# A top-32 attention with two MLPs on one core: K and V buffers assigned by next use, head pairs in alternating order, 28 weight low halves on GpSimd, and the instruction list made by two more backward and forward passes

## The chip, the core and the metric

The kernel runs on one core of one Trainium2 chip. Times are microseconds (us) on the device, from the launch of the program to its end on that core. The median of three runs of the kernel before is 1062.55 us. One further execution was profiled; its own time is 1063.52 us, and the profile's span, from its first to its last instruction, is 1061.7 us.

## The reference

Attention over 4 batches, 8 heads, 576 tokens and 64 columns, in which each query keeps its 32 largest scores; then an MLP with ELU; then a gated MLP whose third product has no nonlinearity behind it.

```python
scores = scale * np.matmul(q, k.transpose(0, 1, 3, 2))
kth = np.partition(scores, -top_k, axis=-1)[..., -top_k:-top_k + 1]
scores = np.where(scores >= kth, scores, -1000000000.0)
...
attn = attn / (np.sum(attn, axis=-1, keepdims=True) + 1e-09)
x = np.matmul(attn, v)                  # to (2304, 512)
h = x @ w_in                            # 512 x 2048
g = np.where(h > 0.0, h, alpha * (np.exp(np.minimum(h, 0.0)) - 1.0))
y = g @ w_out                           # 2048 x 512
h = (y @ w1) * (y @ w2) @ w3            # 512 x 1024 twice, 1024 x 1024
return h @ w_out2                       # 1024 x 512
```

## The kernel before

**Work and tiles.** The 2304 tokens are 18 tiles of 128, taken in 9 chunks of 2. For a chunk, attention goes over the 4 pairs of heads and, within a pair, over the 2 tiles. A step of attention on one tile and pair is: load q (line 288, from 410 on), split it into a high and a low part on ScalarE and GpSimd (L414, L415), score matmuls on TensorE (L435), evacuation by ScalarE (L437), the top 32 on VectorE as four MAX8 and three MATCH_REPLACE8 per head (L445, L447), mask and exponential on ScalarE (L460, L462), split of the probabilities (L470 on ScalarE, L471 on GpSimd), transposes by DMA (L473), the product with V (L488), the division and split (L499 to L509) and a transpose into X (L510). A tile that straddles two batches takes K and V of both.

**The MLPs** of a chunk follow its attention by one chunk. Unit A is x·W_in (L747 to L749, three f16 products for each f32 one: high·high, high·low, low·high), with the ELU on ScalarE and GpSimd (L759 to L771); unit O is g·W_out (L784 to L786); Y evacuates (L796, L797); unit B is the two gated products (L826 to L828) and their product on VectorE (L836 to L852); unit D is the product with W34 = W3·W_out2 (L861 to L863), and the output goes out. W34 is computed once, by the 64 f32 products of L686.

**Weights.** They arrive as 8-byte words and are made f32 by `load64` (two ScalarE steps, L539 and L541, one of VectorE, L540, one of GpSimd, L542). The tensors w12 and w34 serve as landing places before they hold their own weights. `convert` (L561) then splits a 128x512 tile into two f16 halves: the high half always on ScalarE (L566), the low half in a mode that `conv_modes` picks for every tile. In mode P, TensorE forms scaled weight minus high half in PSUM (L578, L579) and VectorE or ScalarE evacuates it (L582). In mode D, VectorE does it in one instruction (L569). Before, W_in and W_out (16 tiles each) are all P with the evacuation on VectorE; W34 (8 tiles) and W12 (16 tiles) are all D.

**K and V.** There are three K buffers (KT) and four V buffers (VV). `att_loads` and `v_loads` take the next buffer in turn. The first time a batch and pair of heads are needed they are loaded raw (kd, vd), converted (K: L357 and L358; V: L379 and L382), and the converted tile is stored to DRAM (KD, VD); every later time it is reloaded from there. Inside a chunk a K tile that still stands in its buffer is not reloaded.

**Order.** No instruction is placed by hand. `Program.op` collects all operations with an engine, an estimated cost and the buffers they read and write. `emit` (L125) then simulates the engines: at each point the engine that is free first takes, of its operations that are ready, the one of lowest rank. The rank comes from a due time, offsets by group (OFF) and the length of the path behind it. Each engine then runs its instructions in the order so found, waiting on semaphores; the SP engine issues all DMAs, also in order.

Of the kernel before, what the change touches and what calls it, by code (L numbers as in the profile page):

```python
# [39 lines left out]
OFF = {":DVE": 13807, "A0:ACT": -12479, "A0:PE": 9089, "A0:POOL": 28926, "A1:ACT": 1887, "A1:PE": 1481, "A1:POOL": -6842, "A2:ACT": 12564, "A2:PE":  # L40
# [53 lines left out]
class Program:  # L94
# [29 lines left out]

    def emit(self):  # L125
        n = len(self.ops)
        succ = [[] for _ in range(n)]
        miss = [0] * n
        for i, o in enumerate(self.ops):
            miss[i] = len(o[3])  # L130
# [857 lines left out]
```

## Time and profile before

| | |
|---|---|
| median of 3 runs (lowest, highest) | 1062.55 us (1062.33, 1064.52) |
| the profiled execution: own time, span | 1063.52 us, 1061.7 us |
| busy in the span: TensorE, VectorE, ScalarE, GpSimd | 978.0, 888.4, 826.1, 695.2 us |
| mean granted TensorE clock | 0.974 |
| moved by DMA | 174.97 MB |

Busy time is the union of an engine's instructions. The granted clock is a share of 2.4 GHz; 0.5 is 1.2 GHz. A stretch A:B runs from A to B in us from the span's start.

### The profile page before, as it was taken

What the parts mean: (1) busy time and instruction counts of PE and PEld (TensorE: products, weight loads), DVE (VectorE), ACT (ScalarE), POOL (GpSimd) and SP (SyncE); (2) the same over time, 40 slices, a digit from 0 to 9 for tenths busy, and PEclk for the clock granted to TensorE, in tenths of its full rate; (3) what the DMA queues carried; (4) which work ended last, traced back from release to release, by engine and by line L of the source; (5) the groups of instructions that cost most, each with busy time, mean ns of one, the idle gap of its engine ahead of it and who ended that gap; (6) DMA issues with size and microseconds to landing.
All of it is one profiled execution on the core that took longest, in us unless ns stands there. A gap on an engine that the chain in (4) does not pass through costs nothing.

```text
span 1061.7 us, 24618 instructions
## 1 busy us (share of the span) xinstructions
PE 978.0 (92%) x9132; PEld 776.7 (73%) x9132; DVE 888.4 (84%) x1968; ACT 826.1 (78%) x1521; POOL 695.2 (65%) x743
## 2 busy tenths in 40 slices
PE   3486998988899999999999999999999999999998
PEld 2334454777787788977888888788778968978875
DVE  4999998999999999999979999997999999710011
ACT  6899987898999767978887788899669877824512
POOL 4968665698478646965884587489457856833702
PEclk9598999999999999999999999999999999999999
DMA  9979997689456985488787536865862663320000
GB/s 356 397 223 289 304 273 171 192 209 236 118 161 153 238 192 120 90 193 212 187 227 174 147 76 176 221 188 140 179 154 65 138 151 70 57 51 21 1 20 20
DMA packets 255384, 174.97 MB, mean 165 GB/s; under 512 B 196640, under 2 KB 223264, under 8 KB 255264
## 3 DMA queue, kind: packets, MB, share of 16 engines
q1 hardware_dynamic: 255264, 173.41, 63.2%
q8 instruction: 71, 1.16, 0.5%
q14 instruction: 49, 0.40, 0.1%
HBM read 104.56 MB, written 21.61 MB: 119 GB/s over the span
## 4 chain that ended last, share of the span: by engine, by line
PE 33%; DVE 26%; ACT 16%; DMA 11%; POOL 6%; issue 6%; SPq 1%; DVEq 0%; ACTq 0%; POOLq 0%
DVE m L445 10%; DVE wk L447 8%; PE psR L826 2%; PE psR L827 2%; PE psR L828 2%; PE psY L784 2%; DMA raw<-kd 2%; PE psY L786 2%; PE psY L785 2%; DMA qr<-qd 2%; DMA pt<-pi 2%; PE psR L747 2%; PE psR L748 2%; PE psR L749 2%; PE psY L686 2%
## 5 line engine op out<-in xcount | busy, mean ns | idle before, releaser
L445 DVE MAX8 m<-wk 128x8 f32<-128x576 f32 x432 | 311.2, 746 | 0.8
L471 POOL TENSOR_TENSOR pi<-s,pi 128x576 f16<-128x576 f32 x144 | 185.9, 1298 | 80.3 <-ACT pi L470 57.1
L447 DVE MATCH_REPLACE8 wk<-m,wk 128x576 f32<-128x576 f32 x288 | 212.3, 740 | 0.0
L747 PE MATMUL psR<-x,win 128*128 128x256 f16 x576 | 157.2, 273 | 5.9 <-ACT t L768 5.6
L785 PE MATMUL psY<-g,wout 128*128 128x256 f16 x576 | 158.1, 275 | 3.3 <-POOL g L771 3.3
L784 PE MATMUL psY<-g,wout 128*128 128x256 f16 x576 | 158.5, 275 | 1.1 <-ACT g L770 1.1
L826 PE MATMUL psR<-x,w 128*128 128x256 f16 x576 | 158.0, 274 | 1.2 <-DVE t L846 0.9
L786 PE MATMUL psY<-g,wout 128*128 128x256 f16 x576 | 158.1, 274 | 0.0
L827 PE MATMUL psR<-x,w 128*128 128x256 f16 x576 | 157.6, 274 | 0.0
L828 PE MATMUL psR<-x,w 128*128 128x256 f16 x576 | 157.5, 273 | 0.0
L749 PE MATMUL psR<-x,win 128*128 128x256 f16 x576 | 157.0, 273 | 0.0
L748 PE MATMUL psR<-x,win 128*128 128x256 f16 x576 | 157.0, 273 | 0.0
L435 PE MATMUL psS<-kt,qh 128*128 128x288 f32 x320 | 111.7, 363 | 19.5 <-ACT s L437 18.4
L460 ACT ACTIVATE s<-s,m 128x576 f32<-128x576 f32 x144 | 108.6, 770 | 23.4 <-DVE m L445 23.2
L437 ACT ACTIVATE s<-psS 128x576 f32<-128x576 f32 (+1 forms) x160 | 102.9, 643 | 16.4 <-PE psS L435 9.7
L445 DVE MAX8 m<-s 128x8 f32<-128x576 f32 x144 | 104.5, 744 | 10.5 <-ACT s L437 10.3
L462 ACT ACTIVATE s<-s,ty 128x576 f32<-128x576 f32 x144 | 106.7, 769 | 4.4 <-POOL ty L456 4.4
L447 DVE MATCH_REPLACE8 wk<-m,s 128x576 f32<-128x576 f32 x144 | 106.1, 740 | 0.0
L470 ACT ACTIVATE pi<-s 128x576 f16<-128x576 f32 x144 | 95.0, 676 | 8.7 <-DMA pt<-pi 8.1
L769 POOL TENSOR_TENSOR t<-t,t 128x512 f32<-128x512 f32 x72 | 92.8, 1290 | 5.5 <-ACT t L768 3.8
L415 POOL TENSOR_TENSOR ql<-qr,qh 128x256 fp32r<-128x256 f32 x72 | 54.1, 752 | 60.8 <-ACT qh L414 57.0
L435 PE MATMUL psS<-kt,ql 128*128 128x288 f32 x320 | 93.4, 305 | 0.1
(155 smaller groups left out, 2382.6 us busy)
## 6 DMA issues: line engine op xcount, KB each, us to landing
kt<-kd SPq DMA_DIRECT2D x32, 576.0 KB, 4.6
vv<-vd SPq DMA_DIRECT2D x32, 455.0 KB, 4.6
qr<-qd SPq DMA_DIRECT2D x72, 128.0 KB, 3.0
raw<-kd SPq DMA_DIRECT2D x32, 288.0 KB, 3.8
kd<-kt SPq DMA_DIRECT2D x16, 576.0 KB, 4.6
w<-w_in SPq DMA_DIRECT2D x16, 512.0 KB, 5.9
w<-w_out SPq DMA_DIRECT2D x16, 512.0 KB, 6.9
w<-w3t SPq DMA_DIRECT2D x16, 512.0 KB, 5.5
```

The lines of the kernel that those rows point to most:

```text
L435: T.matmul(psS[:, half, 0:288], lhsT=L[qs][:, hh], rhs=KT[kk][:, hh, half * 288:half * 288 + 288], start=li == 0, stop=li == 1)
L445: op("DVE", 665, lambda r=r, src=src, m8=m8, hh=hh: V.max(m8[:, hh, 8 * r:8 * r + 8], src), [skey], [mk], p1 + PAR["ot"] * STEP)
L447: op("DVE", 727, lambda r=r, src=src, w=w, m8=m8, hh=hh: V.match_replace(w, m8[:, hh, 8 * r:8 * r + 8], src, -3.0e38), [skey, mk], [k], p1 ...
L471: op("POOL", 1240, lambda Y=Y, PIs=PIs, hh=hh: G.tensor_tensor(PIs[:, hh, S:2 * S], Y[:, hh], PIs[:, hh, 0:S], op=OP.subtract), hks, [pk], ...
L747: T.matmul(o, lhsT=hi(W)[:, cs], rhs=X[:, 0, kd_, 0:N], start=kd_ == 0, stop=False)
L748: T.matmul(o, lhsT=hi(W)[:, cs], rhs=X[:, 1, kd_, 0:N], start=False, stop=False)
L784: T.matmul(o, lhsT=hi(W)[:, cs], rhs=rh, start=ft == 0 and m % 2 == 0, stop=False, skip_group_check=True)
L785: T.matmul(o, lhsT=hi(W)[:, cs], rhs=rl, start=False, stop=False, skip_group_check=True)
L786: T.matmul(o, lhsT=lo(W)[:, cs], rhs=rh, start=False, stop=ft == 15, skip_group_check=True)
L826: T.matmul(o, lhsT=hi(W)[:, cs], rhs=X[:, 0, kd_, 0:N], start=kd_ == 0, stop=False)
L827: T.matmul(o, lhsT=hi(W)[:, cs], rhs=X[:, 1, kd_, 0:N], start=False, stop=False)
L828: T.matmul(o, lhsT=lo(W)[:, cs], rhs=X[:, 0, kd_, 0:N], start=False, stop=kd_ == 3)
```

## The change

1. **Buffers by next use.** A new `plan` walks the known sequence of uses of K and V ahead of time. If a tile still stands in a buffer, it is a hit and nothing is loaded. Else it takes the buffer whose content is needed furthest in the future. Only tiles that will be loaded again are stored.
2. **Pairs in alternating order.** Odd chunks take the four pairs from the last to the first (`snake=1`).
3. **Low halves by GpSimd alone.** A new mode S scales the f32 tile in place on GpSimd and subtracts the high half there. 6 of 16 tiles of W_in, 6 of 16 of W_out, all 8 of W34 and 8 of 16 of W12 take it, 28 in all. The other 20 tiles of W_in and W_out stay P, the other 8 of W12 stay D.
4. **The list.** The forward simulation of `emit` becomes a function. Its result is refined twice: a backward pass from the finish times gives every operation a latest start, and the next forward pass ranks operations by that.
5. All offsets in OFF have other values. The new parameter `blag` is 0, so `hold`, `bprev` and the `Bp` units do nothing here.

```diff
-PAR = dict(hv={}, lv={'wi': 16, 'wo': 16}, whole=(), cd={'wi': [0, 0], 'wo': [0, 0], 'w34': [8, 0], 'w12': [16, 0]}, ...
+PAR = dict(fb=2, snake=1, blag=0, hv={}, lv={'wi': 16, 'wo': 16}, whole=(), cd={'wi': [0, 0, 6], 'wo': [0, 0, 6], 'w34': [0, 0, 8], 'w12': [8, 0, 8]}, ...
...
-OFF = {":DVE": 13807, "A0:ACT": -12479, ...
+OFF = {":DVE": 17768, "A0:ACT": -31993, ...
...
-def conv_modes(n, d, g):
+def conv_modes(n, d, g, s=0):
...
+    for z, mode in ((g, "G"), (s, "S")):
+        free = [i for i in range(n) if m[i] == "P"]
+        for k in range(min(z, len(free))):
+            m[free[k * len(free) // z]] = mode
...
+    def backward(self, succ, fin):
...
+            while wait[e] and wait[e][0][0] <= t:
+                _, i = heapq.heappop(wait[e])
+                heapq.heappush(ready[e], (-fin[i], i))
+            _, i = heapq.heappop(ready[e])
+            eng, cost, fn, deps, pr, lat, lk = self.ops[i]
+            free[e] = t + (max(cost, lat) if e == "SP" else cost)
+            end = free[e] + (1100.0 if e == "SP" else 0.0)
+            late[i] = -end
...
+        cur = self.forward(succ, rank)
+        for _ in range(PAR["fb"]):
+            cur = self.forward(succ, self.backward(succ, cur[2]))
+        self.length, order, _ = cur
...
+    def pairs(c):
+        return range(4) if c % 2 == 0 or not PAR["snake"] else range(3, -1, -1)
+
+    def plan(n, uses):
+
+        last, homes, seen, again, steps = {}, [None] * n, set(), set(), []
+        for i, u in enumerate(uses):
+            for x in u:
+                last.setdefault(x, []).append(i)
+        for i, u in enumerate(uses):
+            for x in u:
+                if x in homes:
+                    steps.append((homes.index(x), "hit"))
+                    continue
+                far = [-1 if h in u else len(uses) + n - k if h is None else min([j for j in last[h] if j > i], default=len(uses)) for k, h in enumerate(homes)]
+                k = far.index(max(far))
+                homes[k] = x
+                if x in seen:
+                    again.add(x)
+                steps.append((k, "again" if x in seen else "first"))
+                seen.add(x)
+        return iter(steps), again
...
     def att_loads(b, p, pr):
-        ks = nxt("k", NK)
-        if ("k", b, p) in seen:
+        ks, how = next(kplan)
+        if how == "hit":
+            return ks
+        if how == "again":
             dma(KT[ks].rearrange("p a s -> p (a s)").bitcast(I32), KD[b, p].bitcast(I32), 128 * S * 8, [("kd", b, p)], [("k", ks)], pr)
             return ks
...
-        dma(KD[b, p], KT[ks].rearrange("p a s -> p (a s)").bitcast(F32), 128 * S * 8, [("k", ks)], [("kd", b, p)], pr + PAR["ost"] * STEP)
+        if (b, p) in kagain:
+            dma(KD[b, p], KT[ks].rearrange("p a s -> p (a s)").bitcast(F32), 128 * S * 8, [("k", ks)], [("kd", b, p)], pr + PAR["ost"] * STEP)
...
-        for pair in range(4):
+        for at, pair in enumerate(pairs(c)):
...
-        if mode == "G":
-            op("ACT", 570, lambda: A.activation(st, st, AF.Copy, scale=s), [sk], skeys, pr)
+        if mode in "GS":
+            if mode == "G":
+                op("ACT", 570, lambda: A.activation(st, st, AF.Copy, scale=s), [sk], skeys, pr)
+            else:
+                op("POOL", 660, lambda: G.tensor_scalar(st, st, s, 1.0, op0=OP.mult, op1=OP.mult), [sk], skeys, pr)
             op("POOL", 1160, lambda: G.tensor_tensor(lo(W[i]), st, hi(W[i]), op=OP.subtract), [*skeys, (nm, i)], [(nm, i, "l")], pr)
             return
```

`v_loads` changes as `att_loads` does. In the lists below a row is a line, an operation and its tiles; L542 of before is L623 of the change, L471 is L552, L415 is L498, L456 is L537, L771 is L855, L762 is L846, L769 is L853; L656 and L657 are the two steps of mode S.

The first place is GpSimd's list before W34 is begun, where the last tiles of W_out become f32 (win, wout, w34: weight tiles; w12: landing place; ql, qh: split q; pi, s: probabilities; ty: thresholds). Before:

```order
L542 TENSOR_TENSOR w34_100<-w34_100,w12_99 128x512 x4
L542 TENSOR_TENSOR wout_98<-wout_98,w12_99 128x512 x2
L415 TENSOR_TENSOR ql1_108<-qr_104,qh1_106 128x256
L471 TENSOR_TENSOR pi0_121<-s0_116,pi0_121 128x576
L542 TENSOR_TENSOR wout_98<-wout_98,w12_99 128x512 x2
L471 TENSOR_TENSOR pi0_121<-s0_116,pi0_121 128x576
L456 TENSOR_TENSOR ty1_147<-m81_143 128x2
L542 TENSOR_TENSOR wout_98<-wout_98,w12_99 128x512 x2
L415 TENSOR_TENSOR ql0_107<-qr_104,qh0_105 128x256
L542 TENSOR_TENSOR wout_98<-wout_98,w12_99 128x512 x5
```

and now:

```order
L498 TENSOR_TENSOR ql1_108<-qr_104,qh1_106 128x256
L623 TENSOR_TENSOR wout_98<-wout_98,w12_99 128x512
L552 TENSOR_TENSOR pi0_121<-s0_116,pi0_121 128x576
L623 TENSOR_TENSOR wout_98<-wout_98,w12_99 128x512
L656 TENSOR_SCALAR win_97<-win_97,sc_96 128x512
L623 TENSOR_TENSOR wout_98<-wout_98,w12_99 128x512
L657 TENSOR_TENSOR win_97<-win_97 128x512
L656 TENSOR_SCALAR win_97<-win_97,sc_96 128x512
```

Between the W_out tiles stand now the low halves of W_in (L656, L657), five such pairs in all with those that follow these rows; a probability split that stood there comes later.

The second place is GpSimd's list near the end of chunk 0's first layer, where W12's last tiles become f32 (pp: its last two landing places; g, t: the ELU's tiles; xt: attention's output). Before:

```order
L542 TENSOR_TENSOR pp_138<-pp_138 128x512
L762 TENSOR_SCALAR t4_131<-t4_131,sc_96 128x512
L771 TENSOR_TENSOR g0_132<-t2_129,g0_132 128x512
L471 TENSOR_TENSOR pi0_121<-s2_118,pi0_121 128x576
L769 TENSOR_TENSOR t4_131<-t4_131,t0_127 128x512
L471 TENSOR_TENSOR pi0_121<-s2_118,pi0_121 128x576
L771 TENSOR_TENSOR g1_133<-t4_131,g1_133 128x512
L542 TENSOR_TENSOR pp_138<-pp_138 128x512
L415 TENSOR_TENSOR ql0_107<-qr_104,qh0_105 128x256
L456 TENSOR_TENSOR ty3_149<-m83_145 128x2
```

and now:

```order
L846 TENSOR_SCALAR t4_131<-t4_131,sc_96 128x512
L853 TENSOR_TENSOR t4_131<-t4_131,t0_127 128x512
L552 TENSOR_TENSOR pi0_121<-s2_118,pi0_121 128x576
L656 TENSOR_SCALAR w12_99<-w12_99,sc_96 128x512
L590 TENSOR_TENSOR xt0_135<-xf0_137,xt0_135 128x128
L623 TENSOR_TENSOR pp_138<-pp_138 128x512
L657 TENSOR_TENSOR w12_99<-w12_99 128x512
L537 TENSOR_TENSOR ty3_149<-m83_145 128x2
L855 TENSOR_TENSOR g0_132<-t2_129,g0_132 128x512
L855 TENSOR_TENSOR g1_133<-t4_131,g1_133 128x512
L656 TENSOR_SCALAR w12_99<-w12_99,sc_96 128x512
```

Low halves of W12 (w12_99 in L656 and L657) follow directly, between the last ELU steps and the next probabilities.

The third place is SP's list while W3 is loaded (qr: query; raw: K or V as it comes; kt, kd0, vv, vd0: converted tiles in SBUF and DRAM; pt, x0: transposes). Before:

```order
L288 DMA qr_104<-qd 128x2x128
L288 DMA kt2_111<-kd0_1_64 128x1152
L473 DMA_TRANSPOSE pt0_122<-pi0_121 128x9x128
L288 DMA raw_101<-vd 128x512
L288 DMA w12_99<-w3t 128x4x256
L288 DMA kd0_3_66<-kt0_109 128x1152
L288 DMA w12_99<-w3t 128x4x256
L288 DMA vv0_112<-vd0_0_79 128x1820
L473 DMA_TRANSPOSE pt0_122<-pi0_121 128x9x128
L288 DMA vd0_3_82<-vv3_115 128x1820
```

and now:

```order
L554 DMA_TRANSPOSE pt1_123<-pi0_121 128x9x128
L337 DMA w12_99<-w3t 128x4x256 x4
L554 DMA_TRANSPOSE pt1_123<-pi0_121 128x9x128
L554 DMA_TRANSPOSE pt0_122<-pi0_121 128x9x128
L337 DMA raw_101<-kd 128x576
L337 DMA w12_99<-w3t 128x4x256
L337 DMA qr_104<-qd 128x2x128
L591 DMA_TRANSPOSE x0_124<-xt0_135 128x2x128
L337 DMA raw_101<-vd 128x640
L337 DMA w12_99<-w3t 128x4x256 x2
L554 DMA_TRANSPOSE pt0_122<-pi0_121 128x9x128
```

The stores and reloads of K and V in between are gone; the W3 pieces follow each other and the transposes more closely.

## Rows read from the trace of the kernel before

**Rows 1.** The page: its head and part 1, busy us (share) xinstructions of each engine.
```profile
span 1061.7 us, 24618 instructions
PE 978.0 (92%) x9132; PEld 776.7 (73%) x9132; DVE 888.4 (84%) x1968; ACT 826.1 (78%) x1521; POOL 695.2 (65%) x743
```

**Rows 2.** Table by stretches (us): length, busy us (xinstructions) of PE, PEld, DVE, ACT, POOL; clock; DMA share, GB/s.
```profile
0.00:195.00 195.00, 147.00 (x713) 78.06 (x714) 177.18 (x377) 164.30 (x292) 128.13 (x129) 0.89 0.93 280
195.00:270.00 75.00, 64.88 (x742) 56.46 (x740) 72.61 (x162) 67.99 (x127) 65.08 (x65) 0.98 0.84 214
195.00:384.00 189.00, 171.06 (x1828) 145.38 (x1826) 182.98 (x398) 170.29 (x315) 140.56 (x145) 0.97 0.76 193
384.00:944.00 560.00, 545.91 (x5682) 464.14 (x5680) 518.58 (x1169) 453.12 (x851) 389.39 (x433) 1.00 0.62 147
944.00:1062.00 118.00, 113.99 (x916) 89.08 (x914) 9.70 (x27) 38.42 (x65) 37.17 (x37) 0.99 0.04 15
40.00:121.00 81.00, 61.36 (x300) 30.53 (x301) 80.58 (x174) 78.13 (x140) 59.05 (x53) 0.83 0.95 294
121.00:195.00 74.00, 69.81 (x325) 36.29 (x325) 71.17 (x152) 58.09 (x107) 44.00 (x48) 0.98 0.87 218
201.00:368.00 167.00, 151.25 (x1608) 128.11 (x1607) 163.39 (x355) 154.69 (x285) 129.60 (x134) 0.98 0.73 183
```

**Rows 3.** Single lines: count, duration ns min/median/max, first and last start us.
```profile
L686 PE MATMUL psY<-w,pp x128: 590/592/1061, 121.1 to 194.3; 128*128 128x512 f32 x128
L747 PE MATMUL psR<-x,win x576: 269/273/286, 194.7 to 999.4; 128*128 128x256 f16 x192
L488 PE MATMUL psA<-vv,pt x2240: 189/193/262, 83.8 to 942.8; 128*128 128x65 f16 x105, 128*128 128x64 f16 x46, 128*64 128x65 f16 x24, 128*64 128x64 f16 x12
L762 POOL TENSOR_SCALAR t<-t,sc x72: 687/695/1284, 201.4 to 1001.5; 128x512 f32<-128x512 f32 x72
```

**Rows 4.** PE in order of time, last chunk of tokens.
```profile
984.03 0.27 PE L784 MATMUL psY<-g,wout 128*128 128x256 f16 x1
984.14 0.27 PE L785 MATMUL psY<-g,wout 128*128 128x256 f16 x1
```

**Rows 5.** Who PE waited for from 384 to 944: us in total, times, longest.
```profile
PE psS L435 <- ACT s L437: 5.0, 9, 1.2
PE psA L488 <- DMA pt<-pi: 4.3, 6, 1.5
```

**Rows 6.** PE in order of time: start us, us, instruction; conversions at half and full clock.
```profile
54.63 1.92 PE L578 MATMUL psY<-win,si 128*128 128x512 f32 x2
56.77 0.60 PE L578 MATMUL psY<-win,si 128*128 128x512 f32 x1
...
117.70 1.10 PE L578 MATMUL psY<-w,si 128*128 128x512 f32 x2
118.86 1.02 PE L578 MATMUL psY<-w,si 128*128 128x512 f32 x2
```

**Rows 7.** Groups of instructions: xcount | busy us, mean ns | idle before.
```profile
L771 POOL TENSOR_TENSOR g<-t,g 128x512 f16<-128x512 f32 x72 | 84.0, 1168 | 8.3 <-ACT g L770 6.5 <-issue 1.3
L762 POOL TENSOR_SCALAR t<-t,sc 128x512 f32<-128x512 f32 x72 | 50.8, 706 | 19.8 <-ACT t L760 19.0
L569 DVE SCALAR_TENSOR_TENSOR w<-w,sc 128x512 f16<-128x512 f32 x21 | 21.5, 1046 | 0.2
L582 DVE CAST win<-psY 128x512 f16<-128x512 f32 x16 | 11.0, 685 | 0.2 <-PE psY L579 0.2
```

**Rows 8.** GpSimd in order of time: the last step of chunk 1's first layer.
```profile
367.76 1.16 POOL L771 TENSOR_TENSOR g<-t,g 128x512 f16<-128x512 f32 x1 [1.34 <-issue]
```

**Rows 9.** The page, part 6, DMA issues: xcount, KB each, median us to landing.
```profile
kt<-kd SPq DMA_DIRECT2D x32, 576.0 KB, 4.6
vv<-vd SPq DMA_DIRECT2D x32, 455.0 KB, 4.6
```

More of the change, by code (lines that the diff above doesn't have):

```diff
@@ L123, in op, with forward @@
         self.groups.append(f"{self.tag}:{eng}")
[L125 removed]
+    def forward(self, succ, rank):
         n = len(self.ops)
[L127 to L130, printed above, removed]
[L131 to L137 removed]
+        miss = [len(o[3]) for o in self.ops]
         engs = sorted({o[0] for o in self.ops})
@@ L182, in emit @@
                 end = free[e] = t + cost
+            fin[i] = end
             for s in succ[i]:
@@ L187, in emit @@
                     heapq.heappush(wait[self.ops[s][0]], (rt[s], s))
+        return max(free.values()), order, fin
+    def backward(self, succ, fin):
+        n = len(self.ops)
+        miss = [len(s) for s in succ]
+        engs = sorted({o[0] for o in self.ops})
+        free = {e: 0.0 for e in engs}
+        wait = {e: [] for e in engs}
+        ready = {e: [] for e in engs}
+        rt = [0.0] * n
+        late = [0.0] * n
+        for i in range(n):
+            if miss[i] == 0:
+                heapq.heappush(wait[self.ops[i][0]], (0.0, i))
+        for _ in range(n):
+            best = None
+            for e in engs:
+                if ready[e]:
+                    t = free[e]
+                elif wait[e]:
+                    t = max(free[e], wait[e][0][0])
+                else:
+                    continue
+                if best is None or t < best[0]:
+                    best = (t, e)
+            t, e = best
+            while wait[e] and wait[e][0][0] <= t:
[6 more added lines that the diff above has]
+            late[i] = -end
+            for d in deps:
+                de = self.ops[d][0]
+                rt[d] = max(rt[d], end + (900.0 if de == "SP" else LAT.get((de, eng), 130.0)))
+                miss[d] -= 1
+                if miss[d] == 0:
+                    heapq.heappush(wait[de], (rt[d], d))
+        return late
@@ new lines, in emit @@
+    def emit(self):
+        n = len(self.ops)
+        succ = [[] for _ in range(n)]
+        for i, o in enumerate(self.ops):
+            for d in o[3]:
+                succ[d].append(i)
+        cp = [0.0] * n
+        for i in range(n - 1, -1, -1):
+            e, c = self.ops[i][:2]
+            cp[i] = c + max([cp[s] + (2050.0 if e == "SP" else LAT.get((e, self.ops[s][0]), 130.0)) for s in succ[i]], default=0.0)
+        rank = [o[4] - PAR["cpw"] * cp[i] for i, o in enumerate(self.ops)]
+        cur = self.forward(succ, rank)
+        for _ in range(PAR["fb"]):
+            cur = self.forward(succ, self.backward(succ, cur[2]))
+        self.length, order, _ = cur
@@ L188, in emit @@
         order.sort()
-        self.length = max(free.values())
-        self.busy = {e: sum(o[1] for o in self.ops if o[0] == e) for e in engs}
+        self.busy = {e: sum(o[1] for o in self.ops if o[0] == e) for e in {o[0] for o in self.ops}}
         for _, i in order:
@@ L344 @@
     op("DVE", 135, consts, [], ["ident", ("xf", 0), *[(k, i) for k in ("v", "vl") for i in range(NV)]], -1e6)
+    def pairs(c):
[9 more added lines that the diff above has]
+                    steps.append((homes.index(x), "hit"))
+                    continue
+                far = [-1 if h in u else len(uses) + n - k if h is None else min([j for j in last[h] if j > i], default=len(uses)) for k, h in enumerate(homes)]
[6 more added lines that the diff above has]
+        return iter(steps), again
+    starts = [sum(chunks[:i]) for i in range(len(chunks))]
+    kuse, vuse = [], []
+    for c_, n_ in enumerate(chunks):
+        for p_ in pairs(c_):
+            for t_ in range(starts[c_], starts[c_] + n_):
+                kuse.append([(b_, p_) for b_ in range(t_ * 128 // S, (t_ * 128 + 127) // S + 1)])
+            vuse.append([(b_, p_) for b_ in sorted({starts[c_] * 128 // S, ((starts[c_] + n_) * 128 - 1) // S})])
+    kplan, kagain = plan(NK, kuse)
+    vplan, vagain = plan(NV, vuse)
     def att_loads(b, p, pr):
-        ks = nxt("k", NK)
-        if ("k", b, p) in seen:
+        ks, how = next(kplan)
+        if how == "hit":
+            return ks
+        if how == "again":
             dma(KT[ks].rearrange("p a s -> p (a s)").bitcast(I32), KD[b, p].bitcast(I32), 128 * S * 8, [("kd", b, p)], [("k", ks)], pr)
             return ks
-        seen.add(("k", b, p))
         for hh in range(2):
@@ L877, in mlp @@
         dp = list(dprev)
+        seq += [("Bp", b) for b in bprev]
         if dp:
@@ L882, in mlp @@
             seq.append(("Dp", dp.pop(0)))
-        for j in range(8):
-            seq.append(("B", j))
+        if not hold:
+            for j in range(8):
+                seq.append(("B", j))
         for kind, i in seq:
             pr = pr_of(u)
-            c_ = c - (kind == 'Dp')
+            c_ = c - (kind in ("Dp", "Bp"))
             P.tag = f"{kind[0]}{c_ if c_ < 4 or c_ > len(chunks) - 3 else chr(115)}"
@@ L900, in mlp @@
                 i(pr)
-                u += 1
+                u += kind == "Dp"
             u += kind != "Y"
-        return [lambda pr, t=t: unitD(t, pr) for t in range(n)]
-    starts = [sum(chunks[:i]) for i in range(len(chunks))]
+        ds = [lambda pr, t=t: unitD(t, pr) for t in range(n)]
+        return (ds, [lambda pr, j=j: unitB(j, pr) for j in range(8)]) if hold else ds
     prep_v(0, PAR["pv"] * STEP)
@@ L911 @@
     st12 = prep_12(PAR["p12"] * STEP)
+    done12 = []
     def hooks(kind, i):
-        if kind == "Y":
+        if not done12 and (kind == "Bp" or kind == "Y" and not PAR["blag"]):
+            done12.append(1)
             for f in finish_12(st12, (PAR["p12"] + 16 * PAR["p12s"]) * STEP):
                 f()
-    dprev = []
+    dprev, bprev = [], ()
     for c, n in enumerate(chunks):
@@ L929 @@
             banks[:] = [0, 1] if c == 1 else [0, 1, 2]
-            dprev = mlp(c - 1, starts[c - 1], m, dprev, (starts[c] * 8 + PAR["lag0" if c == 1 else "lag"]) * STEP, m * 8 * STEP, hooks if c == 1 else None)
+            banks[:] = [0, 1] if c == 1 + PAR["blag"] else banks
+            hold = c == 1 and PAR["blag"] == 1
+            dprev = mlp(c - 1, starts[c - 1], m, dprev, (starts[c] * 8 + PAR["lag0" if c == 1 else "lag"]) * STEP, m * 8 * STEP, hooks if c < 3 else None, bprev, hold)
+            bprev = ()
+            if hold:
+                dprev, bprev = dprev
     c = len(chunks) - 1
```

51 lines of the change are left out of this document (20 added, 31 removed), and 56 rows, old and new, of the table OFF.

## Prediction

> **What bounds the kernel now.** I read the page first [rows 1]: TensorE (PE) is busy 978.0 of 1061.7 us, VectorE (DVE) 888.4, so no share of busy time decides by itself; the stages must be taken apart. The table by stretches does that [rows 2], with the cuts at the milestones of [rows 3]: the first product W3·W4 at 121.1, the first matmul of chunk 0's MLP at 194.7, the last attention product at 942.8.
> - 384 to 944: PE is busy 545.9 of 560, DVE 518.6. The f16 matmuls start 0.11 us apart although each row says 0.27 [rows 4]; they overlap, and "busy" here means that the next is already queued. PE is the limit, DVE close behind. PE idles 14.1 us; its two largest waits there are for score evacuations (5.0) and for the transposes of the probabilities (4.3) [rows 5].
> - 944 to the end: attention is over, PE works off what is queued, 114.0 of the last 117.7 us.
> - 0 to 195: PE has 48 us of idle time. From 40 to 121 DVE is busy 80.6 of 81 and ScalarE (ACT) 78.1, while GpSimd (POOL) has 22 us free and the TensorE clock is granted at 0.83 on average, so part of it at 1.2 GHz. DVE and ACT pace the weight conversion, and with it the start of everything.
> - 195 to 384: all four are loaded. PE idles 17.9, DVE 6.0, ACT 18.7, POOL 48.4.
>
> So the end moves by what comes off PE's work plus what changes in PE's idle time. A microsecond of PE work removed in the front counts only if DVE and ACT let PE use it.
>
> The Trainium skill's page "Perfetto Trace Analysis" (Identifying the Most-Contended Engine) says that matmul occupancy does not measure how full TensorE is. By that alone 92% would prove no bound, and PE work taken away might be worth nothing, which is the first rival's time; the overlap in [rows 4] shows why the page warns, and the even spacing there is why I keep the bound.
>
> **The change, part by part.**
> *28 low halves.* Twelve leave PE and DVE: a conversion on PE is a pair of f32 passes and one f16 matmul, and the next begins 1.16 us later at full clock (117.70 to 118.86), 2.14 at half (54.63 to 56.77) [rows 6]. 12 x 1.16 = 13.9 us of PE work go (25.7 if all ran at half clock). DVE loses 12 evacuations of 0.69 and 16 direct low halves of 1.05 [rows 7]: 8.2 + 16.7 = 24.9 us. POOL gains 28 pairs; the scaling has the shape of L762 (0.71), the subtraction that of L771 (1.17) [rows 7]: 28 x 1.87 = 52.5 us. The shortest and longest L762, 0.69 and 1.28 [rows 3], bound a pair between 1.86 and 2.45, so 52 to 69. I take 52.5, since the median is at the low end.
>
> *Front, to the first W3·W4 product.* In the new lists ACT has 14 attention and K/V instructions fewer and 3 weight instructions more ahead of the second W3 piece: 11 x 0.56 (78.13 us over 140 instructions [rows 2]) = 6.1 us. DVE sheds more (the 12 evacuations alone are 8.2), so ACT decides. POOL has 10 pairs more there, 18.7 us, less six attention or K instructions that now come later; its 22 free us hold that. I take **-6**. Of the 13.9 us off PE the other 8 become idle time. Ends: 0 (if another wait takes over) and -13.9. The block of 64 products that follows is PE-bound (busy 69.8 of 74 from 121 to 195 [rows 2]), so it moves as a whole. The lists have the same 27 score steps, 8 attention products and all but one W3·W4 product ahead of the first MLP matmul, so nothing else is owed at that point.
>
> *195 to 384.* 16 pairs (29.9 us) fall between the first POOL step of chunk 0's MLP and the last of chunk 1's first layer, from 201 [rows 3] to 368 [rows 8], where POOL has 37.4 us free [rows 2]. They replace DVE's 16.7 us. DVE is the fuller engine here, and the score and attention work waits on it. I let PE's 17.9 idle us fall by **4**; ends -17.9 and, if POOL cannot fit the work, the second rival below.
>
> *K and V.* K reloads fall from 32 to 12 and K stores from 16 to 12; V reloads from 32 to 6 and V stores from 16 to 6. A store carries the same tile as a reload; by the sizes in [rows 8], 24 x 576 + 36 x 455 KB = 30.9 MB no longer move. Transposes share the engines with them, and PE waits 4.3 us for transposes after 384. The two passes over the list aim at the same idle time. Together **-3** from 384 to 944; ends 0 and -9.3, the sum of the two waits in [rows 5]. The new wait: all reloads still wait for the last score step on their buffer, SP issues in order, and a late one holds up the query loads and transposes queued behind it. One reload lands in 4.6 us [rows 9]; a K tile serves two query tiles, so one wait that long is covered while the other tile's top-32 runs. I cost it at nothing and leave it to the second rival's side of the range.
>
> *Tail.* Seven of the D steps (six matmuls each) now stand ahead of the last attention product; this shifts work, PE stays full, 0.
>
> **Sum.** Own time of the profiled execution 1063.5 - 6 - 4 - 3 = 1050.5. The median of the runs is 1.0 lower, so **1049.5**. The ends of the terms add up to 1021 below and, with the second rival, 1070 above; they would all have to fall together.
>
> **Rivals.**
> 1. *Nothing reaches the end.* The front is paced by ACT, which loses no instruction at all, and the freed PE time is all idle. If more conversions fall into stretches at 1.2 GHz, as part of 40 to 121 is now, each costs 0.98 more and eats up the rest. For: 78.1 of 81 busy. Against: the list in front of the W3 pieces is shorter on ACT and DVE both. Time 1062.
> 2. *POOL becomes the limit* between the first and second chunk's first layer. In 201 to 368 POOL works 129.6; with 29.9 more it is 159.5. In 195 to 270, when it always had work, it was busy 65.1 of 75, 87%. At that rate 159.5 takes 184 us, 17 more than now; 6 earlier at the start and 3 recovered later leave +8: **1070**. It decides once POOL cannot hold 159.5/173 = 92%. For: POOL waits mostly for ACT, which is just as full. Against: a low half waits only for its high half, so it fills gaps. The Trainium skill's "GPSIMD Engine Reference" (Engine selection) speaks for this rival: it wants elementwise work with two inputs on VectorE, as GpSimd needs about twice as long. The rows agree in direction (1.17 against 0.69 in [rows 7], with other operands): on the engines' own clocks the change pays 52.5 us for 24.9 plus 13.9, a loss wherever POOL is what the others wait for.
> 3. *The passes do more than I grant.* Half of PE's 32 idle us after 195 vanish and all 13.9 us of PE work come off: 1062.5 - 13.9 - 16 = 1033. For: the new list interleaves finer. Against: PE stands at 97% after 384 already.
> That the change does not do what it says is closed: the instruction counts above are from the lists.
>
> **Numbers.** About 0.2%, 2.1 us, is what a measurement of this kernel can tell from no change. The forecast has 0.70 (1037 to 1059), the first rival 0.10, the second 0.09, the third 0.11. The range 1036 to 1063 leaves out the second rival and about two thirds of the third. Faster: 0.70 + 0.11, less a little at the edge, 0.80; same 0.10; slower 0.10.
>
> **What would show it.** Right: 20 conversions on PE; the first W3·W4 product near 115 and the first MLP matmul near 188; POOL over 90% busy for the 160 us after that with PE no more idle than before; last attention product near 939, and from there some 9 us less to the end, for the seven D steps. Wrong: the first MLP matmul still at 194 (first rival); PE or ACT waiting for GpSimd's low halves or for the subtraction of g around 270 to 370 (second); PE idle below 10 us between 384 and 944 (third).

## The result and the profile after

| | before | the change |
|---|---|---|
| median of 4 runs each (lowest, highest) | 1062.44 us (1061.1, 1064.52) | 1047.1 us (1044.43, 1049.93) |
| ratio, 95% interval | | 0.9854 [0.9821, 0.9888] |
| profiled execution: own time, span | 1063.52, 1061.7 us | 1045.63, 1043.9 us |
| mean granted TensorE clock of it | 0.974 | 0.993 |

The time fell by 15.3 us; 13.0 were forecast (from 1062.55 to 1049.5), and 1047.1 lies inside the range. The reasons given for it hold much less well, as the stages and the experiments show.

The page of the change, head and part 1, against [rows 1]:

```profile
span 1043.9 us, 24535 instructions
PE 962.5 (92%) x9096; PEld 769.2 (74%) x9096; DVE 868.9 (83%) x1940; ACT 823.3 (79%) x1521; POOL 744.0 (71%) x799
```

TensorE (PE) has 15.5 us less work and only 2.3 us less idle time (1043.9 - 962.5 = 81.4 against 83.7). VectorE (DVE) lost 19.5 us, GpSimd (POOL) gained 48.8; 24.9 and 52.5 were estimated.

The milestones of [rows 3] have moved to (count, shortest, median and longest in ns, first and last start in us; L770 was L686, L831 was L747, L569 was L488):

```profile
L770 PE MATMUL psY<-w,pp x128: 590/592/697, 107.8 to 188.1; 128*128 128x512 f32 x128
L831 PE MATMUL psR<-x,win x576: 269/273/421, 185.1 to 976.3; 128*128 128x256 f16 x192
L569 PE MATMUL psA<-vv,pt x2240: 189/193/242, 82.4 to 934.0; 128*128 128x65 f16 x105, 128*128 128x64 f16 x46, 128*64 128x65 f16 x26, 128*64 128x64 f16 x10
```

The table by stretches with the cuts at these milestones, and the 160 us that the prediction named (columns as in [rows 2]):

```profile
0.00:107.80 107.80, 61.58 (x286) 33.37 (x286) 93.58 (x195) 94.01 (x162) 91.33 (x91) 0.97 0.86 292
107.80:185.10 77.30, 71.47 (x389) 37.45 (x388) 75.97 (x164) 66.55 (x127) 55.93 (x61) 1.00 0.91 213
185.10:372.90 187.80, 170.66 (x1825) 144.40 (x1823) 182.33 (x406) 174.13 (x322) 171.64 (x179) 0.98 0.64 164
372.90:934.00 561.10, 552.68 (x5718) 468.15 (x5716) 506.55 (x1148) 450.98 (x848) 388.05 (x432) 1.00 0.51 114
934.00:1043.90 109.90, 106.09 (x891) 85.82 (x887) 10.45 (x30) 37.59 (x65) 37.08 (x37) 1.00 0.04 14
185.00:345.00 160.00, 144.66 (x1515) 122.89 (x1514) 156.12 (x350) 151.00 (x276) 149.71 (x154) 0.98 0.64 164
```

The same cuts in the trace of before, stretches 1 to 3:

```profile
0.00:121.10 121.10, 77.30 (x391) 41.87 (x392) 106.11 (x226) 106.31 (x186) 84.23 (x82) 0.83 0.96 318
121.10:194.70 73.60, 69.41 (x322) 35.95 (x321) 70.77 (x152) 57.73 (x106) 43.60 (x48) 0.98 0.87 218
194.70:383.30 188.60, 170.66 (x1823) 145.02 (x1821) 182.58 (x396) 170.15 (x314) 140.86 (x146) 0.97 0.76 193
```

| stretch | before, us | change, us | difference | forecast |
|---|---|---|---|---|
| 1: start to the first W3·W4 product | 121.1 | 107.8 | -13.3 | -6 |
| 2: to the first MLP matmul of chunk 0 | 73.6 | 77.3 | +3.7 | 0 |
| 3: to the first matmul of chunk 1's gated products | 188.6 | 187.8 | -0.8 | -4 |
| 4: to the last attention product | 559.5 | 561.1 | +1.6 | +6 (-3, and 9 for seven D steps) |
| 5: to the end | 118.9 | 109.9 | -9.0 | -9 (the seven D steps) |

At the end of stretch 3 both kernels have issued the same PE work (248 score matmuls and 27 attention products among it) apart from the 12 conversions, so the first three rows together are a true gain of 10.4: PE's work up to there fell by 13.7 us and its idle time rose by 3.3. The last two rows must be read together, since seven D steps changed sides: -7.4.

Who PE waited for in stretch 4 (total us, times, longest), against [rows 5]:

```profile
PE psA L569 <- DMA pt<-pi: 3.7, 4, 2.0
PE psR L910 <- DVE t L930: 1.7, 4, 0.6
PE psY L888 <- DVE x L881: 0.9, 2, 0.7
```

The waits for score evacuations, 5.0 in [rows 5], are gone from the list, those for the transposes fell from 4.3 to 3.7.

Part of the difference between the two profiled executions may be the clock. Of 45 timed executions of the kernel before, beside the experiments below, 5 had a mean granted clock under 0.98; their median is 1065.6 us, that of the other 40 is 1063.3. The profiled one, with 0.974, took 1063.5. So at most about 2.3 of the 17.8 us by which the spans differ (an estimate from these medians) belong to the clock of that one execution; the medians of the two kernels differ by 15.3.

In the prediction's part on K and V the sizes named with [rows 8] stand in [rows 9].

### The profile page after: what moved, and what is told of

Read it like the earlier page. It is cut to its first block, busy times and chain, and to the rows that moved or that the text cites. A ratio compares the mean times of both kernels' runs of the same rounds, so it can differ in the third digit from the quotient of the medians.

```text
span 1043.9 us, 24535 instructions
## 1 busy us (share of the span) xinstructions
PE 962.5 (92%) x9096; PEld 769.2 (74%) x9096; DVE 868.9 (83%) x1940; ACT 823.3 (79%) x1521; POOL 744.0 (71%) x799
## 3 DMA queue, kind: packets, MB, share of 16 engines
q8 instruction: 71, 1.16, 0.5%
## 4 chain that ended last, share of the span: by engine, by line
DVE 39%; PE 25%; ACT 17%; DMA 7%; issue 7%; POOL 5%; SPq 0%; POOLq 0%; DVEq 0%; ACTq 0%
DVE m L526 18%; DVE wk L528 15%; PE psR L910 2%; PE psR L912 2%; PE psR L911 2%; DMA pt<-pi 2%; ACT psR L620 2%; PE psR L831 2%; PE psR L833 2%; PE psR L832 2%; DMA w<-w3t 2%; ACT s L518 2%; ACT pi L551 2%; PE psY L869 1%; PE psY L870 1%
## 5 line engine op out<-in xcount | busy, mean ns | idle before, releaser
L552 POOL TENSOR_TENSOR pi<-s,pi 128x576 f16<-128x576 f32 x144 | 184.7, 1289 | 75.6 <-ACT pi L551 56.9
L831 PE MATMUL psR<-x,win 128*128 128x256 f16 x576 | 157.9, 274 | 4.3 <-ACT t L852 3.5
L516 PE MATMUL psS<-kt,qh 128*128 128x288 f32 x320 | 108.7, 355 | 10.1 <-ACT s L518 7.6
L853 POOL TENSOR_TENSOR t<-t,t 128x512 f32<-128x512 f32 x72 | 92.8, 1290 | 2.4 <-ACT t L852 0.8
L855 POOL TENSOR_TENSOR g<-t,g 128x512 f16<-128x512 f32 x72 | 84.8, 1180 | 8.2 <-ACT g L854 7.8
```

Of the source, the lines that this page charges most:

```text
L516: T.matmul(psS[:, half, 0:288], lhsT=L[qs][:, hh], rhs=KT[kk][:, hh, half * 288:half * 288 + 288], start=li == 0, stop=li == 1)
L552: op("POOL", 1240, lambda Y=Y, PIs=PIs, hh=hh: G.tensor_tensor(PIs[:, hh, S:2 * S], Y[:, hh], PIs[:, hh, 0:S], op=OP.subtract), hks, [pk], ...
L831: T.matmul(o, lhsT=hi(W)[:, cs], rhs=X[:, 0, kd_, 0:N], start=kd_ == 0, stop=False)
```

## The experiments

`emit` also gives the length that its own simulation expects (`self.length`). It is no time of the chip, but it is what the offsets in OFF can be fitted to; it is called the planned length below. Before has 1043.3, the change 1033.6. PE busy and idle are of one profiled execution each (idle is the span less busy).

| kernel | ratio to before, 95% interval | median, us | planned, us | PE busy, idle, us |
|---|---|---|---|---|
| before | 1 | 1062.4 | 1043.3 | 978.0, 83.7 |
| the change | 0.9854 [0.9821, 0.9888] | 1047.1 | 1033.6 | 962.5, 81.4 |
| no_s | 0.9987 [0.9975, 0.9998] | 1061.9 | 1053.9 | 982.8, 76.7 |
| turn | 0.9979 [0.9959, 0.9999] | 1062.6 | 1044.9 | 971.9, 88.8 |
| no_refine | 1.0108 [1.0092, 1.0125] | 1075.2 | 1063.1 | 969.2, 103.8 |
| old_off | 1.0127 [1.0107, 1.0147] | 1077.8 | 1067.5 | 974.3, 105.6 |
| passes_unfit | 0.9934 [0.9912, 0.9955] | 1057.2 | 1042.9 | 975.1, 81.0 |
| fit_passes | 0.9862 [0.9834, 0.9891] | 1048.9 | 1033.4 | 971.9, 73.2 |
| fit_no_s | 0.9815 [0.9790, 0.9840] | 1044.2 | 1032.8 | 970.0, 71.2 |
| fit_turn | 0.9890 [0.9867, 0.9914] | 1052.6 | 1031.6 | 964.2, 86.2 |
| fit_all | 0.9858 [0.9835, 0.9881] | 1049.3 | 1034.1 | 962.1, 84.6 |
| fit_all2 | 0.9787 [0.9763, 0.9811] | 1041.1 | 1031.6 | 958.0, 81.8 |
| fit_early | 0.9821 [0.9796, 0.9846] | 1044.9 | 1030.4 | 960.5, 81.0 |
| fit_w34 | 0.9742 [0.9717, 0.9766] | 1036.6 | 1030.9 | 969.7, 63.6 |

### One part of the change undone, offsets kept

**no_s**, the conversion modes of before:

```diff
-cd={'wi': [0, 0, 6], 'wo': [0, 0, 6], 'w34': [0, 0, 8], 'w12': [8, 0, 8]}
+cd={'wi': [0, 0, 0], 'wo': [0, 0, 0], 'w34': [8, 0, 0], 'w12': [16, 0, 0]}
```

> The change with the conversion modes of before (W_in and W_out all P, W34 and W12 all D); buffers, pair order, refinement and offsets as in the change. Theory A (the gain of the front comes from the work that the 28 low halves take off PE and DVE): the first W3.W4 product comes back to 117 to 122 us and the time rises by 8 to 14, to 1055 to 1061. Theory B (the gain of the front comes from the new list and the missing DMAs, the low halves only change places): first product at 107 to 112, time within 3 us of the change, 1044 to 1050.

Measured: 1061.9, with the first product at 119.1. By the numbers theory A has it, though the time lies 0.9 above its range. But the front is only part of it, as the stretches show (stretches 1 and 2 in one row, then 3, 4 and 5):

```profile
0.00:191.00 191.00, 147.41 (x707) 76.95 (x708) 171.91 (x352) 160.50 (x286) 126.21 (x126) 0.97 0.84 253
191.00:376.70 185.70, 169.02 (x1764) 143.70 (x1763) 182.15 (x406) 168.30 (x309) 140.53 (x142) 0.97 0.63 157
376.70:949.70 573.00, 560.29 (x5781) 474.30 (x5781) 522.04 (x1182) 459.57 (x864) 390.60 (x438) 0.99 0.48 114
949.70:1059.50 109.80, 106.06 (x890) 85.79 (x886) 10.44 (x30) 37.50 (x65) 37.06 (x37) 0.99 0.04 14
```

Of the 15.6 us of span 5.9 are lost at the first MLP matmul, with PE busy 147.4 against 133.0 and less idle than in the change. Stretch 3 is 2.1 shorter. The rest, 11.9, is in stretch 4, 573.0 against 561.1, where no weight is converted: it takes over 8 score matmuls and 2 attention products that stretch 3 of the change had done, and PE idles 12.7 against 8.4. So this run does not separate the low halves from the fit of the list.

**turn**, buffers in turn and pairs always 0 to 3:

```diff
-PAR = dict(fb=2, snake=1, ...
+PAR = dict(fb=2, snake=0, ...
...
-    kplan, kagain = plan(NK, kuse)
-    vplan, vagain = plan(NV, vuse)
+    kplan, kagain = turn(NK, kuse)
+    vplan, vagain = turn(NV, vuse)
```

`turn` gives each new tile the next buffer, calls a tile a hit only within one chunk's pair, and has all tiles stored.

> The change with K and V buffers taken in turn, a reload whenever a pair of a new chunk begins, all converted tiles stored, and the pairs always in the order 0 to 3 (32 K reloads, 16 K stores, 32 V reloads, 16 V stores again). Theory A (the 30.9 MB hid well; what they cost is waits of PE for transposes and K): plus 1 to 5 us, 1048 to 1052, all of it after 384. Rival (transfers that no longer run free the SP queue in the front as well): plus 6 or more, with the first product late by 3 or more.

Measured: 1062.6, 15.5 above the change, where theory A had 1 to 5; the first product came at 114.7, 6.9 late. By the numbers the rival has it.

**no_refine**, the first list as it is:

```diff
-PAR = dict(fb=2, ...
+PAR = dict(fb=0, ...
```

> The change with fb=0, so the first list of the simulation is used as it is. Theory A (the list passes only trim waits of PE; in the sum they share a term of 3 us with the buffers): 1048 to 1051, the front's first product within 3 us of 107.8. Theory B (the passes make most of the front's gain): 1055 or more, first product at 114 or later.

Measured: 1075.2, slower than before by 1.1%; first product at 118.6. Theory A is out by 24 us; by the numbers theory B has it.

**old_off**, the offsets of before:

```diff
-OFF = {":DVE": 17768, "A0:ACT": -31993, "A0:PE": 5415, ...
+OFF = {":DVE": 13807, "A0:ACT": -12479, "A0:PE": 9089, ...
```

> The change with the offsets of before in OFF; everything else as in the change. The offsets were not a term of the sum. Theory A (after two passes over the list the first ranks matter little): within 4 us of the change, 1044 to 1051. Rival (the offsets carry the gain): 1055 or more.

Measured: 1077.8; by the numbers the rival has it. The offsets, which are not a term of the sum, cost 31 us when they are the wrong ones.

**What follows.** By the medians the four losses are 15, 16, 28 and 31 us, 90 together (83 by the ratios, which set each run against before in its own round), for a change that brought 15. They can't be the worth of the parts. All four planned lengths rose too, from 1033.6 to 1044.9 and more. The offsets are fitted to one set of operations; take any part away and one measures the misfit with it. So each part was tried again with offsets of its own.

### The same parts, each with offsets fitted to it

All four start from the offsets of before. Random trials change the offsets, some 260 in number, and keep what shortens the planned length; 80000 trials each. The diff of each is that of the namesake above, and OFF.

> The change with the offsets of before as the start, and 80000 random trials on the offsets that keep what shortens the length that the list's own simulation gives (it ends at 1034.1; the change has 1033.6, before 1043.3). Control for the next three, which had the same start and trials. Theory A and theory B: 1045 to 1051. If it comes out above 1055, offsets fitted this way are worth less than those of the change, and the four runs can be compared only with each other.

> As fit_all, with the conversion modes of before (own fit, simulated length 1032.8). Theory A (the low halves taken off PE and DVE carry the front's gain): 8 to 14 us above fit_all, first W3.W4 product at 117 or later. Theory B (the 15 us of the run without them came from offsets that belong to another set of operations; the refined list makes up for the work): within 4 us of fit_all.

> As fit_all, with K and V buffers in turn, all stores and reloads, pairs in the order 0 to 3 (own fit, simulated length 1031.6). Theory A (the 30.9 MB hide well): 1 to 5 us above fit_all. Theory B (nothing but the list counts): within 2 us. A third theory (the list's simulation knows too little of the DMAs, so transfers cost more on the chip than in it): 6 or more above fit_all.

> The kernel before (its modes, buffers and pair order) with only the two backward and forward passes, own fit of the offsets (simulated length 1033.4). Theory A (low halves 10 us, passes and buffers 3): 1058 to 1062. Theory B (the passes with fitted offsets carry the gain): 1046 to 1052.

**fit_passes** against before:

```diff
+PAR = dict(fb=2, ...
-OFF = {":DVE": 13807, "A0:ACT": -12479, "A0:PE": 9089, ...
+OFF = {":DVE": -365183, "A0:ACT": -476671, "A0:PE": -9978, ...
```

The control **fit_all** came to 1049.3, within the scatter of the change; so offsets found in this way are as good as those of the change. **fit_passes**, which has none of the low halves on GpSimd, no planned buffers and no alternating order, gives 0.9862 where the change gives 0.9854. The two passes, with offsets that suit them, are enough for a gain as large as the whole; theory B. No run fits the offsets without the passes, so what such a fit alone would give is open. Nor is it the same gain: the first MLP matmul of fit_passes comes at 194.4, as before (194.7), where the change has 185.1. The page and stretches 3 and 4 of fit_passes:

```profile
span 1045.1 us, 24644 instructions
PE 971.9 (93%) x9132; PEld 773.4 (74%) x9132; DVE 887.8 (85%) x1968; ACT 824.5 (79%) x1521; POOL 698.6 (67%) x743
```

```profile
194.40:372.00 177.60, 166.09 (x1766) 140.74 (x1765) 172.72 (x379) 165.01 (x305) 141.45 (x141) 0.99 0.75 197
372.00:950.30 578.30, 570.73 (x5924) 484.40 (x5922) 529.35 (x1197) 462.35 (x870) 397.33 (x443) 1.00 0.61 146
```

PE's instructions are those of before; it is busy 6.1 us less (at a mean clock of 0.993 in place of 0.974), and 10.5 us of its idle time are gone: 11.5 idle in stretch 3 (before 17.9), 7.6 in stretch 4 (before 14.1).

**fit_no_s** is not 8 to 14 us slower than fit_all but 5 faster, outside both theories. Without the 28 low halves on GpSimd PE works longer and waits less (first fit_no_s, then fit_all):

```profile
span 1041.2 us, 24556 instructions
PE 970.0 (93%) x9132; PEld 773.8 (74%) x9132; DVE 889.1 (85%) x1968; ACT 825.1 (79%) x1521; POOL 697.7 (67%) x743
```

```profile
span 1046.7 us, 24517 instructions
PE 962.1 (92%) x9096; PEld 773.7 (74%) x9096; DVE 870.2 (83%) x1940; ACT 824.2 (79%) x1521; POOL 744.0 (71%) x799
```

970.0 busy and 71.2 idle, against 962.1 and 84.6 in fit_all. The first product came at 117.4 (114.8 in fit_all), the first MLP matmul at 188.7 (187.2): the front is hardly longer with the 12 conversions back on PE.

fit_passes and fit_turn differ by the low halves alone as well, here with the buffers in turn. With the low halves on GpSimd the time is 3.7 us longer (1052.6 against 1048.9), PE busy 7.8 us less and idle 13.0 more. But in this pair the front did get shorter, by 8.9 us (up to the first MLP matmul, first fit_passes, then fit_turn):

```profile
0.00:194.40 194.40, 144.10 (x705) 76.00 (x706) 178.06 (x375) 163.57 (x290) 126.31 (x128) 0.97 0.93 279
0.00:185.50 185.50, 131.04 (x671) 71.14 (x671) 170.75 (x357) 160.64 (x287) 147.50 (x151) 0.96 0.98 293
```

What was won there was lost later: in stretch 3 PE idles 18.6 us in fit_turn and 11.5 in fit_passes, of which 10.6 and 3.2 go to waits for ScalarE's evacuation of scores.

**fit_turn** lies 3.3 us above fit_all, inside theory A's 1 to 5, though its planned length is 2.5 shorter. fit_passes against fit_no_s is the same comparison without the low halves, and gives 4.7. So both pairs speak for some 3 to 5 us from the planned buffers and the alternating order, which the planned length does not see; two lists of one program can differ by more (fit_all2 below), so their worth is not shown. Which wait they shorten is not shown either: PE's waits for transposes in stretch 4 are no longer in fit_turn (2.9 us) than in fit_all (4.7).

### The passes alone, and the low halves one group at a time

**passes_unfit** is before with `fb=2` and nothing else.

> The kernel before with the two backward and forward passes and nothing else: its own offsets, not fitted again (simulated length 1042.9, before 1043.3). If the passes by themselves make the gain: 1046 to 1052, as in fit_passes. If it takes passes and offsets fitted to them together: 1058 to 1064.

Measured: 1057.2, between the two: the passes bring 6.7 us at a planned length that is unchanged, fitted offsets the other 8.

**fit_all2** is fit_all after 300000 further trials.

> fit_all with 300000 further trials (simulated length 1031.6 in place of 1034.1, now below the 1032.8 of fit_no_s). If fit_all lay 5 us above fit_no_s for want of fitting: 1042 to 1045. If the 28 low halves themselves cost (freed PE time becomes idle time, GpSimd fuller): 1046 to 1050.

Measured: 1041.1, 8.2 us below fit_all, from 2.5 us of planned length; 0.9 under the range for want of fitting, and clear of the other. fit_no_s has not had these further trials. So two lists of the same program can differ on the chip by some 6 us more than they should, and a difference of 5 us between two fitted kernels, such as fit_no_s and fit_all, is not by itself the worth of a part.

**fit_early**, mode S on the 12 tiles that leave PE, and **fit_w34**, mode S on the 8 tiles of W34 (both with buffers, order and passes of the change, and offsets of their own; how many trials these two had is not known here, and their planned lengths are 2.4 and 1.9 us shorter than that of fit_no_s):

```diff
-cd={'wi': [0, 0, 6], 'wo': [0, 0, 6], 'w34': [0, 0, 8], 'w12': [8, 0, 8]}
+cd={'wi': [0, 0, 6], 'wo': [0, 0, 6], 'w34': [8, 0, 0], 'w12': [16, 0, 0]}
```

```diff
-cd={'wi': [0, 0, 6], 'wo': [0, 0, 6], 'w34': [0, 0, 8], 'w12': [8, 0, 8]}
+cd={'wi': [0, 0, 0], 'wo': [0, 0, 0], 'w34': [0, 0, 8], 'w12': [16, 0, 0]}
```

> fit_no_s with mode S on 6 tiles each of W_in and W_out only, the 12 that leave PE; W34 and W12 all D (own fit, simulated length 1030.4). If the PE work taken off the front counts: 8 to 14 us below fit_no_s, 1030 to 1036. If it turns into idle time of PE: within 3 us of fit_no_s, 1041 to 1047, with PE busy 7 to 10 us less from the start to the first MLP matmul and that matmul at the same time within 3 us.

> fit_no_s with mode S on the 8 tiles of W34 only, so nothing leaves PE, DVE loses 8 direct low halves (8.4 us) and GpSimd gains 15 us (own fit, simulated length 1030.9). If DVE's relief counts where it is the fuller engine (term of 4 us for 16 such tiles): 2 us or more below fit_no_s, at most 1042. If not: within 2 us of it or above.

The page of fit_early:

```profile
span 1041.5 us, 24514 instructions
PE 960.5 (92%) x9096; PEld 770.9 (74%) x9096; DVE 883.9 (85%) x1956; ACT 823.9 (79%) x1521; POOL 717.4 (69%) x767
```

PE lost 9.5 us of work against fit_no_s and got 9.8 us of idle time; the ratio is 0.9821 against 0.9815. The first MLP matmul came at 179.1, earlier than expected, but with 114 of the 128 W3·W4 matmuls behind it instead of all; the last of them started at 197.7, and the 14 that were owed are 6.8 us of PE's work. Part of the idle time is in the conversions that are left: PE waits for the scale matrices and for evacuations, both on DVE. First fit_early up to its first MLP matmul, then fit_no_s (who PE waited for, total us, times, longest; L640 makes a scale matrix, L666 evacuates; each is one line less in fit_no_s):

```profile
PE psY L662 <- DVE si L640: 9.9, 2, 5.7
PE psY L662 <- DVE wout L666: 5.1, 2, 4.7
```

```profile
PE psY L661 <- DVE si L639: 2.1, 2, 1.8
PE psY L661 <- DVE wout L665: 1.9, 4, 0.7
```

The page of fit_w34, and its stretch 3 beside that of fit_no_s (first fit_w34, then fit_no_s):

```profile
span 1033.3 us, 24561 instructions
PE 969.7 (94%) x9132; PEld 773.5 (75%) x9132; DVE 882.8 (85%) x1960; ACT 827.5 (80%) x1521; POOL 708.9 (69%) x759
```

```profile
190.00:359.10 169.10, 159.60 (x1671) 135.97 (x1670) 168.23 (x371) 162.47 (x298) 149.66 (x153) 1.00 0.63 164
```

```profile
188.70:366.50 177.80, 163.52 (x1764) 140.07 (x1763) 176.59 (x392) 166.38 (x307) 142.60 (x142) 1.00 0.67 163
```

It is the fastest of all, 1036.6 us or 0.9742 [0.9717, 0.9766], 1.1% below the change. PE's work is that of fit_no_s; its idle time is 63.6 us, less than in any other kernel here, and 9.5 in stretch 3 against 14.3 (the stretch holds 93 PE instructions fewer here). DVE has 8 direct low halves less in the kernel. The direction is that of the term for 195 to 384. Whether the 7.6 us belong to the 8 low halves is open after fit_all and fit_all2; there is one list of each, and the fits may not have had the same number of trials.

## Why the prediction was right, and where its reasons were not

**The number** was right: 1049.5 against 1047.1, ratio 0.9854 [0.9821, 0.9888]. That is partly luck: by stage the sum missed by 7.3 and 4.4 us one way and by 3.7 and 3.2 the other. And it was not right for its reasons: it gave 10 of 13 us to the low halves and 3 to buffers and passes together; the runs give the passes with offsets fitted to them a gain as large as all of it (0.9862), buffers and order 3 to 5 us, and the 28 low halves as a whole 5 and 4 us of loss (fit_all against fit_no_s, fit_turn against fit_passes) or 3 of gain (fit_all2, with more trials, against fit_no_s), less than two lists of one program differ by. What share of the change's own 15 us each part brought stays open, since the parts do not add up.

**The step that failed: "*Front, to the first W3·W4 product* ... I take -6"**, as the worth of the low halves, and beside it "together -3" for buffers and passes. What failed is the reasoning that what the low halves give in the front reaches the end: in the change's own list it did, in three fitted pairs it did not. The time to that product did fall, by twice as much as forecast, 13.3 us. ACT's work ahead of it fell from 106.3 to 94.0 us and DVE's from 106.1 to 93.6, with 162 ACT instructions in place of 186. I had counted to the second W3 piece, where 11 are missing; to the product itself it is 24. But part of that work was only put off: the block of 64 products that "moves as a whole" grew by 3.7. PE had 389 instructions in it in place of 322 and was busy 2.1 us longer; DVE's work in it rose from 70.8 to 76.0 and ACT's from 57.7 to 66.6.

The first MLP matmul still came 9.6 us earlier. With fitted lists that differ by the modes alone it comes 1.5 us earlier (fit_no_s to fit_all) or 8.9 (fit_passes to fit_turn), and the whole time is longer by 5.1 and 3.7; fit_early gains 9.6 there, 6.8 of PE's work being owed, and ends where fit_no_s does. PE idles longer in stretch 3 in all three (fit_all 17.5, fit_turn 18.6 and fit_early 17.9 us, against 14.3, 11.5 and 14.3), and its waits for ScalarE's evacuation of scores are longer there in all three (7.5, 10.6 and 5.4 us against 3.6, 3.2 and 3.6). Why ScalarE is later with them is not shown.

**12 conversions off PE**, estimated at 13.9 us of PE work: PE's busy time fell by 9.5 between fit_no_s and fit_early. The conversions' own instructions fell from 50.7 to 36.5 us, as estimated; the rest of PE's work took longer. The first rival's claim, that the freed PE time is all idle, fits these two lists: 9.8 us more idle. Its signs did not show in the change itself, where the first MLP matmul came at 185.1 and PE's idle time fell by 2.3. The Trainium skill's "Perfetto Trace Analysis" (Identifying the Most-Contended Engine) says that matmul occupancy is no good measure of how close a kernel is to TensorE's limit. That PE work taken away might therefore be worth nothing was my inference; for these 12 conversions fit_early and fit_no_s agree with it, one list each. I had granted 6 us to the front against it.

**28 pairs on GpSimd**, 52.5 us: the durations were right. The groups in the change (count | busy us, mean ns | idle before; L650 is the direct low half, L666 the evacuation of a conversion):

```profile
L657 POOL TENSOR_TENSOR w<-w 128x512 f16<-128x512 f32 x14 | 17.2, 1234 | 0.2
L657 POOL TENSOR_TENSOR win<-win 128x512 f16<-128x512 f32 x5 | 5.8, 1160 | 0.0
L656 POOL TENSOR_SCALAR w<-w,sc 128x512 f32<-128x512 f32 x16 | 12.0, 748 | 2.3 <-ACT w L647 2.2
L656 POOL TENSOR_SCALAR win<-win,sc 128x512 f32<-128x512 f32 x5 | 3.4, 691 | 0.0
L650 DVE SCALAR_TENSOR_TENSOR w<-w,sc 128x512 f16<-128x512 f32 x7 | 7.0, 1003 | 0.0
L666 DVE CAST win<-psY 128x512 f16<-128x512 f32 x10 | 6.8, 680 | 0.0
```

All L656 and L657 of the page's groups add up to 53.8 us.

**195 to 384, "-4"**: measured -0.8. POOL was busy 149.7 of 160 us (93.6%), with PE idle 17.1 us against 17.9, just what the text named as the sign of being right, and the 87% that the second rival took as POOL's rate was no limit; but PE's idle time was also to fall by 4, and it did not. No wait of PE for a GpSimd low half shows, and ACT waits 0.4 us for one; the second rival's +8 did not come. Relief for DVE may still be worth something: fit_w34 has 9.5 us of PE's idle time in this stretch, but one list does not show it. The Trainium skill's "GPSIMD Engine Reference" (Engine selection) prefers VectorE for elementwise work with two inputs, since GpSimd takes about twice as long. The rows above agree for the pair (0.69 + 1.16 us on GpSimd against 1.00 for the one instruction on DVE), and less for the step with two inputs alone (1.16). That the time suffers does not follow where DVE is the fuller engine: the pairs of fit_w34 take 15.7 us on GpSimd, DVE is busy 6.3 us less than in fit_no_s, and it is the fastest.

**384 to 944, "together -3"**: -7.4. The direction and the place were right, PE's idle time fell from 14.1 to 8.4 and the score waits went. The size was not: the passes by themselves bring 6.7 us (passes_unfit) and 14.7 with fitted offsets (1 - 0.9862 of 1063.9), and the buffers perhaps another 3 to 5. The transfers that went are as counted (DMA issues of the change: count, KB each, median us to landing; the reloads of before in [rows 9]):

```profile
kd<-kt SPq DMA_DIRECT2D x12, 576.0 KB, 4.1
kt<-kd SPq DMA_DIRECT2D x12, 576.0 KB, 4.4
vd<-vv SPq DMA_DIRECT2D x6, 455.0 KB, 4.4
vv<-vd SPq DMA_DIRECT2D x6, 455.0 KB, 4.3
```

**Offsets at nothing.** The prediction gave the new numbers in OFF no term. They cost 31 us in the wrong place (old_off), and 8 of the gain (passes_unfit to fit_passes).

**Tail**: -9.0 for the seven D steps, as said. **Third rival** (the passes do more): its sign showed, since PE idles 8.4 us between 384 and 944, under the 10 that the prediction named. fit_passes goes the same way: PE's idle time from its first MLP matmul on is 22.9 us, 12.9 less than before. Its size did not come: PE's idle time after 195 fell by 6.4 us, far from half of 32.

## What to carry to other kernels

When a list is fitted to a program, undoing one part measures the misfit of the list together with the part: here four such losses add up to 90 us for a gain of 15. Fit each variant anew, with the same start and number of trials, and take a second list of one program to learn how much the list alone scatters (here 8 us). Work taken off the engine that bounds the kernel can come back as idle time, also in a later stretch, as it did in fit_early, fit_all and fit_turn; compare its busy and idle time together, and to the end, before you credit it.

## What the runs showed of the hardware

Where work has left PE in the front, the granted clock is often lower. In fit_early, where 12 conversions are gone from PE, it was granted at 0.69 and 0.79 on average in these two stretches, so for a part of each at 1.2 GHz, with PE busy 24.0 of 36 and 25.3 of 40 us and DVE busy nearly throughout (the clock is the third number from the end of a row):

```profile
36.00:72.00 36.00, 23.98 (x99) 12.33 (x100) 36.00 (x73) 35.82 (x63) 35.77 (x34) 0.69 0.93 301
70.00:110.00 40.00, 25.30 (x139) 14.16 (x138) 39.41 (x77) 34.48 (x62) 34.52 (x33) 0.79 0.69 197
```

The mean clocks of the timed runs mostly go the same way: 0.972 to 0.985 in fit_early, 0.977 to 0.988 in fit_all and fit_all2, but 0.990 to 0.995 in fit_w34 and 0.982 to 0.995 in fit_no_s, which convert on PE. It is no rule: the change itself had 0.986 to 0.993, and no_s, which converts on PE, 0.981 to 0.988. What remains on PE is slower at the lower level, 2.14 us for a conversion in place of 1.16 [rows 6]. The 20 conversions left in fit_early took 1.82 us of PE each on average, the 32 of fit_no_s 1.58, so 4.8 us come back.

The planned length is only a rough guide: the chip took 5.6 us more than planned for fit_w34, 13.5 for the change, 19.1 for before and 21.0 for fit_turn. So a difference of a few us between two planned lengths says little, as fit_turn shows, which is planned 2.5 us shorter than fit_all and is 3.3 longer.
